# Casts of the down weights behind the last sine of the newest chunk, and last stores split by channel halves

## The chip, the cores and the metric

The kernel runs on one core of one Trainium2 chip. The metric is device time in microseconds from one launch to its end; a kernel's time is the median of its runs. The core has five engines that run side by side, each with its own instruction order: TensorE (matmul; weight loads are listed apart as PEld), VectorE (DVE), ScalarE (ACT), GpSimd (POOL) and SyncE (SP), which here only issues DMA transfers. ACT and POOL issue transfers too. Engines wait for each other through semaphores.

## The reference, cut to what matters

The input `x` has 2048 tokens of 448 channels. After a layer norm two branches are computed and added to `x`: a state-space convolution over the tokens (by FFT), and a gated linear unit.

```python
def _A_ref(u, log_A_real, A_imag, C_real, C_imag, log_dt, D_skip):
    dt = jnp.exp(log_dt)
    A = -jnp.exp(log_A_real) + 1j * A_imag
    C = (C_real + 1j * C_imag) * dt[:, None]
    P = jnp.exp((A * dt[:, None])[:, :, None] * pos[None, None, :])
    K = 2.0 * jnp.einsum("dn,dnl->dl", C, P).real
    Kf = jnp.fft.rfft(K, L2)
    Uf = jnp.fft.rfft(u_t, L2)
    y = jnp.fft.irfft(Uf * Kf[None, :, :], L2)[:, :, :L]
    return y + u * D_skip[None, None, :]

def _B_ref(x, w_gate, w_up, w_down):
    g = jnp.einsum("bsd,df->bsf", x, w_gate)
    u = jnp.einsum("bsd,df->bsf", x, w_up)
    h = _sigmoid(g) * u
    return jnp.einsum("bsf,fd->bsd", h, w_down)

xn = _layernorm(x, axis=-1)
return x + _A_ref(xn, ...) + _B_ref(xn, B_w_gate, B_w_up, B_w_down)
```

The hidden width of the gated unit is 1792, that is 14 tiles of 128, called f = 0 to 13 below.

## The kernel before, in words

Two Python generators write the program. `conv()` makes the convolution branch: norms and transposes of `x`, then `prep`, then `kgen` (the convolution kernel, in 56 chunks of 8 channels), then `spectra` (the products in the frequency domain and the way back). `glu()` makes the gated unit. The last lines of `s4d_glu_kernel` advance the generator that has done the smaller share of its total; a generator hands back, at each `yield`, how much work it counts. That gives the order in which instructions are traced. A scheduler then writes each engine's own order: among the instructions whose inputs are there it prefers those traced earlier. `hp(HP)` gives the instructions of a block a preference as if they had been traced 300 earlier. `tc.issue_after(ins)` puts what its block traces on the engine of `ins` behind `ins` in that engine's order; what the block traces on other engines is left alone.

**The gated unit.** Tokens go in two halves of 1024, each as two tiles `t` of 512. The f are taken in groups of 3, 3, 3, 3 and 2. For each f and t, `gate` multiplies the tokens by the gate and up weights (L709, each weight and input in a high and a low part: `wh`, `wl`, `xh`, `xl`; 11 matmuls for the gate and 11 for the up product), takes the tanh on ACT (`th`, L717, kept in `marks[0]`), multiplies on VectorE (`hf`, L720) and splits the result into `hh` (ACT, L725) and `hl` (VectorE, L727). At t = 0 the down weights of f are made ready. In the first half they are loaded (`rd`), rounded to the high part `dh` by a cast on ACT (L785), and POOL takes the rest `dl = rd - dh` (L786). The tiles that the second half will need again are stored by SyncE, except those of the f in `RAW` (f = 0, 1, 2, 4, 5). In the second half `dh` and `dl` come from there, or are made on POOL alone.

When all f of a group have been through their gates, 8 output blocks of 128 tokens follow (L825): three matmuls for each f, `hh` x `dh`, `hh` x `dl`, `hl` x `dh`, accumulated in one bank `po`, which VectorE adds to `acc` (L830). The banks of the gates (`gu`) and of the output blocks (`po`) share one tag with four buffers.

**The chunks.** `ahead(cn)` makes the phases of a chunk: two matmuls into `tr` (L542), then on ACT an absolute value (L548) and three sines (L549, L550, L551), into `S`. The last of them, L551, is kept in `sins`. POOL makes the magnitudes `me` and `mf` (L508, L520), VectorE multiplies them with the sines (`Et`, `Ft`, L602 to L604), and TensorE sums over the states (`ko`, L616). Chunk cn + 1's phases are traced ahead of chunk cn's products. The phases of chunk 0 are traced with high preference before the loop.

**The order around the change.** Run by the shares, the two generators trace the first `ahead` just before the cast of f = 5. For the casts of f = 5 to 13 the chunk traced last is 0, 0, 2, 5, 10, 12, 15, 20 and 22.

**The end.** The last group of the second half stores the output as it becomes ready. `out(src, b0, nb, ds, engs)` stores `nb` blocks from `b0`, channels `ds`, in four transfers (one for each 32 partitions), given in turn to the queues `engs`. `accs[2]` holds the blocks 8 to 11 and `accs[3]` (also `acc` at t = 1) the blocks 12 to 15. `H` is 224, half of the channels; `last(1, m)` adds the convolution's second half of channels to the output tiles, and at b = 3 that happens just ahead of the last stores.

Of the kernel before, what the change touches and what calls it, by code (L numbers as in the profile page):

```python
# [20 lines left out]
D = 448  # L21
# [15 lines left out]
HP = 300  # L37
Y0 = (8, 1)
CP = D // 4
H = D // 2  # L40
# [91 lines left out]
def s4d_glu_kernel(ctx, tc, io):  # L132
    nc = tc.nc
    hp = tc.high_priority
# [95 lines left out]
    accs = [acc_tile() for _ in range(2)]  # L230
# [230 lines left out]
    def kgen(pk):  # L461
# [73 lines left out]
        def ahead(cn):  # L535


            S = tl[f"S{cn % 2}"]
            ps = psc[-1].tile([128, 2, 512], F32, name="tr", bufs=1)
            ph = pht[cn // 2 % 2]  # L540
            for h in range(2):
                nc.tensor.matmul(ps[:, h], ph[:, cn % 2, 128 * h : 128 * h + 128], sel, start=True, stop=True)  # L542
            if cn % 2 == 1 and cn + 3 < NCK:
                phase_load(cn // 2 + 2)
            rows = lambda t: t.rearrange("p c (h e) s -> p h c (e s)", h=2)
            pv = ps.rearrange("p h (c x) -> p h c x", c=2)
            cs = S[:, 1:4:2]
            nc.scalar.activation(rows(cs), pv, AF.Abs)  # L548
            nc.scalar.activation(rows(S[:, 0:5:4]), pv, AF.Sin, scale=TWO_PI)  # L549
            nc.scalar.activation(rows(S[:, 2:3]), pv[:, :, 0:1], AF.Sin, scale=-TWO_PI)  # L550
            sins[:] = [nc.scalar.activation(cs, cs, AF.Sin, scale=-TWO_PI, bias=hpi)]  # L551
            return S

        def first_stage(bank):
# [175 lines left out]
    def glu():  # L730
        for half in range(2):
# [4 lines left out]
            for fs_ in ORDER[half]:  # L736
                fc, f0 = len(fs_), fs_[0]
                wts, ws, hs = [], [], [[], []]
                cross = half == 0 and fs_ is ORDER[0][-1]
                final = half == 1 and fs_ is ORDER[1][-1]  # L740

                order = [(f, t) for t in range(2) for f in fs_] if cross else [(f, t) for f in fs_ for t in range(2)]
                if half == 0 and f0 == 0:
                    order[1], order[2] = order[2], order[1]
                if cross:
                    xts = {b: pair_load(b) for b in range(8, 16, 2)}
                    step = lambda f_, b: f_(b, xts[b])
                    mid = [(pair_norm, 8), None, (pair_first, 8), (pair_first, 10)]
                    end = [(), ((pair_turn, 8), (pair_norm, 10)), ((pair_turn, 10), (pair_norm, 12)), ((pair_turn, 12), (pair_norm, 14))]
                    downs = {(0, 0): (pair_first, 12), (0, 1): (pair_turn, 14), (0, 3): (pair_first, 14)}  # L750
                for n_, (f, t) in enumerate(order):
                    if t == 0:
                        wh = pg.tile([128, 2, 4, 128], F32R, name="wh", bufs=2)
                        if half == 0:
                            first = len(raws) == 2
                            raw, rd = raws.pop() if raws else (w_load(f), None)
                            wl = w_low()
                            with hp(HP):
                                nc.scalar.copy(wh, raw)
                                if first:  # L760
                                    v.scalar_tensor_tensor(wl, raw, lim[:, 0, 0:1], wh, ALU.mult, ALU.subtract)
                                else:
                                    v.tensor_tensor(wl, raw, wh, ALU.subtract)
                            if f not in RAW:
                                for t_, d_ in kept((wh, wl), wt_d, f):
                                    nc.sync.dma_start(d_, t_)
                        elif f in RAW:
                            raw, wl = w_load(f, eng=nc.gpsimd), w_low()
                            nc.gpsimd.tensor_copy(wh, raw)  # L769
                            nc.gpsimd.tensor_tensor(wl, raw, wh, ALU.subtract)  # L770
                        else:
                            wl = w_low()
                            for t_, d_ in kept((wh, wl), wt_d, f):
                                nc.sync.dma_start(t_, d_)
                        ws.append((wh, wl))
                    between = (lambda s_=mid[n_]: step(*s_)) if cross and mid[n_] else None

                    yield from gate(ws[f - f0], xq[2 * half + t], hs[t], between, half == 0 and (f, t) == (1, 0))
                    if t == 0:
                        dh = pg.tile([128, D], F32R, name="dh", bufs=FCH[0])  # L780
                        if half == 0:
                            rd = rd or rd_load(f)
                            dl = d_low()
                            with hp(HP), tc.issue_after((act if f == 1 else marks)[0].ins):
                                nc.scalar.copy(dh, rd)  # L785
                            nc.gpsimd.tensor_tensor(dl, rd, dh, ALU.subtract)  # L786
                            if f not in RAW:
                                for t_, d_ in kept((dh, dl), dt_d, f):
                                    nc.sync.dma_start(d_, t_)
                        elif f in RAW:  # L790
                            dl = d_low()
                            rd = rd_load(f, pg.tile([128, D], F32, name="rdw", tag="wraw", bufs=1), nc.gpsimd)
                            nc.gpsimd.tensor_copy(dh, rd)  # L793
                            nc.gpsimd.tensor_tensor(dl, rd, dh, ALU.subtract)  # L794
                        else:
                            dl = d_low()
                            for t_, d_ in kept((dh, dl), dt_d, f):
                                nc.sync.dma_start(t_, d_)
                        wts.append((dh, dl))
                    yield 2.5  # L800
                    for s_ in end[n_] if cross else ():
                        step(*s_)
                    if cross:
                        yield 2
                for t in range(2):
                    acc = accs[2 * half + t]
                    for b in range(4):
                        if final and (t, b) == (0, 1):

                            yield None  # L810
                        if final and t == 1 and b >= 2:

                            sp_mm[:] = glu_mm
                            for m in (4 * b - 8, 4 * b - 6):
                                lasts[0](1, m)
                            if b == 3:
                                out(accs[2], 8, 4, slice(H, D), (nc.sync, nc.scalar))
                                out(accs[3], 12, 3, slice(0, D), (nc.sync, nc.scalar))
                        po = psg.tile([128, D], F32, name="po", tag="gu", bufs=4)
                        bs = slice(128 * b, 128 * b + 128)  # L820
                        n = 0
                        with tc.issue_after(sp_mm[0].ins) if glu_on else nullcontext():
                            for (hh, hl), (dh, dl) in zip(hs[t], wts):
                                for a_, w_ in ((hh, dh), (hh, dl), (hl, dh)):
                                    glu_mm[:] = [nc.tensor.matmul(  # L825
                                        po, a_[:, bs], w_, start=(n == 0), stop=(n == 3 * fc - 1)
                                    )]
                                    n += 1
                        with hp(HP):
                            v.scalar_tensor_tensor(  # L830
                                acc[:, b], po, 0.5, acc[:, b], ALU.mult, ALU.add
                            )
                        yield 0.6 * fc
                        if cross and (t, b) in downs:
                            step(*downs[t, b])
                    if cross:
                        nc.sync.dma_start(acc_d[:, 4 * t : 4 * t + 4], acc)
                    if final and t == 0:
                        out(acc, 8, 4, slice(0, H), (nc.gpsimd,))
                    elif final:  # L840
                        out(acc, 15, 1, slice(0, D), (nc.sync, nc.scalar))

    def spectra(pf):

# [260 lines left out]
        with tc.tile_pool(name="pf", bufs=1, side="right", reuse_waits="tile") as pf:  # L1105
            yield from spectra(pf)

    turns = []
    lasts, glu_mm, sp_mm, glu_on, x1s, hfs, xls = [], [], [], [], [0], [], []
    xq, psc, raws, acl, marks, slots, pqs = list(x_first), [], [], [], [None, None], {}, []  # L1110
    W1s, GGs, act, exps = [], [], [], []
# [43 lines left out]
```

## Time and profile before

| | us |
|---|---|
| median of 3 runs | 711.02 (710.64 to 714.73) |
| the profiled execution | 710.54 |
| its span, first to last instruction | 708.8 |
| mean granted TensorE clock | 0.988 of full speed |

The page gives for each engine its busy time and its share of the span. A row of the timeline has the start, the duration, the engine, the line of the kernel, the operation, the tiles written and read, their sizes, how many instructions the row merges, and in brackets the engine's idle time before them with the instruction that ended it. A row for a stretch of time has the busy time of TensorE, weight loads, VectorE, ACT and POOL, the granted clock, the share of the DMA engines and GB/s.

### The profile page before, as it was taken

The numbers are of one execution on the slowest core, as the hardware profiler recorded it, in microseconds if no ns is written. First come the engines' busy times: TensorE is split into PE (matmuls) and PEld (weight loads), VectorE is DVE, ScalarE is ACT, GpSimd is POOL, SyncE is SP. The second block draws the span as 40 slices with busy tenths as digits, with TensorE's granted clock in tenths as the row PEclk, the third lists the DMA queues.
The fourth block names the chain that finished last, engine by engine and source line by source line (L and its number), as shares of the span: only waits on it lengthen the run. The fifth ranks groups of instructions, "written<-read, shape, count | busy, mean of one in ns | idle before, by whom it ended". The sixth has DMA issues, their size and how long they took to land. (4 is left out here: it accounts for less than half of the span.)

```text
span 708.8 us, 19098 instructions
## 1 busy us (share of the span) xinstructions
PE 668.1 (94%) x7752; PEld 523.7 (74%) x7752; DVE 555.7 (78%) x766; ACT 428.7 (60%) x678; POOL 384.9 (54%) x433
## 2 busy tenths in 40 slices
PE   2798999999999998999999999999999999999996
PEld 2575878878877875756878878877777777777784
DVE  5899987699899998898478899988946555566544
ACT  3656965578689779877577788778543322322320
POOL 2101227655999999777446698798765001344001
PEclk9999999999999998989999999999999999999999
DMA  9956274554253544546833333242269988999756
GB/s 200 239 149 204 70 230 150 170 183 132 63 169 135 169 123 135 162 146 202 258 112 103 92 112 108 68 138 82 54 179 280 257 236 238 266 272 221 182 146 182
DMA packets 93031, 117.22 MB, mean 165 GB/s; under 512 B 12240, under 2 KB 76624, under 8 KB 92944
## 3 DMA queue, kind: packets, MB, share of 16 engines
q1 hardware_dynamic: 65376, 91.75, 46.3%
q10 hardware_dynamic: 24896, 18.13, 8.7%
q0 software_dynamic: 2672, 6.13, 3.2%
q8 instruction: 61, 1.00, 0.6%
q14 instruction: 26, 0.21, 0.1%
HBM read 72.13 MB, written 43.84 MB: 164 GB/s over the span
## 5 line engine op out<-in xcount | busy, mean ns | idle before, releaser
L520 POOL TENSOR_TENSOR me<-me,pm 128x32 f32<-128x32 f32 (+1 forms) x168 | 154.9, 922 | 66.8 <-DVE Et L603 38.1
L520 POOL TENSOR_TENSOR mf<-mf,pm 128x64 f32<-128x64 f32 (+1 forms) x112 | 116.9, 1044 | 5.1
L709 PE MATMUL gu<-xh,wh 128*128 128x512 f32 x336 | 100.1, 405 | 3.8 <-DVE acc L830 1.6
L709 PE MATMUL gu<-xh,wl 128*128 128x512 f32 x336 | 96.9, 393 | 0.0
L709 PE MATMUL gu<-xl,wh 128*128 128x512 f32 x336 | 95.1, 390 | 0.0
L602 DVE TENSOR_TENSOR Et<-me,S 128x1024 f32<-128x1024 f32 x56 | 80.2, 1433 | 11.6 <-ACT S L551 10.3
L825 PE MATMUL po<-dh,hh 128*128 128x448 f32 x224 | 84.2, 376 | 3.1 <-ACT hh L725 1.9
L548 ACT ACTIVATE S<-tr 128x1024 f32<-128x1024 f32 x56 | 57.7, 1030 | 44.9 <-PE tr L542 41.0
L604 DVE TENSOR_TENSOR Ft<-mf,S 128x1024 f32<-128x1024 f32 x56 | 80.1, 1431 | 5.3 <-PE ko L616 3.7
L603 DVE TENSOR_TENSOR Et<-me,S 128x1024 f32<-128x1024 f32 x56 | 80.4, 1436 | 4.8 <-ACT me L533 4.5
L825 PE MATMUL po<-dh,hl 128*128 128x448 f32 x224 | 82.4, 369 | 0.3 <-DVE hl L727 0.3
L825 PE MATMUL po<-dl,hh 128*128 128x448 f32 x224 | 82.3, 368 | 0.0
L709 PEld LDWEIGHTS gu<-xh,wh 128*128 128x128 f32 x336 | 60.8, 189 | 24.2 <-issue 4.4
L709 PEld LDWEIGHTS gu<-xh,wl 128*128 128x128 f32 x336 | 63.4, 189 | 14.7 <-DVE ve L255 0.7
L709 PEld LDWEIGHTS gu<-xl,wh 128*128 128x128 f32 x336 | 63.0, 188 | 13.5
L725 ACT CAST hh<-hf 128x512 fp32r<-128x512 f32 x56 | 34.9, 623 | 62.4 <-DVE hf L720 61.4
L616 PEld LDWEIGHTS ko<-Et,Ft 128*32 128x32 f32 x3584 | 54.7, 112 | 24.2 <-issue 13.4
L720 DVE SCALAR_TENSOR_TENSOR hf<-th,gu 128x512 f32<-128x512 f32 x56 | 38.1, 680 | 39.9 <-PE gu L709 35.2
L786 POOL TENSOR_TENSOR dl<-rd,dh 128x448 fp32r<-128x448 f32 x14 | 25.6, 1830 | 78.8 <-ACT dh L785 68.5
L616 PE MATMUL ko<-Et,Ft 128*32 128x64 f32 x3584 | 65.2, 223 | 2.6 <-DVE Ft L604 2.4
L551 ACT ACTIVATE S<-S,hpi 128x1024 f32<-128x1024 f32 x56 | 65.5, 1170 | 0.0
L717 ACT ACTIVATE th<-gu 128x512 f32<-128x512 f32 x56 | 33.5, 599 | 49.4 <-PE gu L709 43.0
(208 smaller groups left out, 1318.0 us busy)
## 6 DMA issues: line engine op xcount, KB each, us to landing
sk_d<-sk ACTq DMA_DIRECT2D x14, 512.0 KB
sx<-x_d SPq DMA_DIRECT2D x32, 224.0 KB
skl<-sk_d SPq DMA_DIRECT2D x16, 448.0 KB
vp<-v_d SPq DMA_DIRECT2D x16, 448.0 KB
v_d<-vt SPq DMA_DIRECT2D x14, 448.0 KB
ph<-ph_d SPq DMA_DIRECT2D x224, 24.0 KB
wt_d<-wh SPq DMA_DIRECT2D x9, 512.0 KB
wt_d<-wl SPq DMA_DIRECT2D x9, 512.0 KB
```

The lines of the kernel that those rows point to most:

```text
L520: ins = nc.gpsimd.tensor_tensor(m[:, :, w + a : 2 * w : n], m[:, :, a:w:n], par(base + i).unsqueeze(2).to_broadcast([128, 4 * DC, w // n]) ...
L548: nc.scalar.activation(rows(cs), pv, AF.Abs)
L551: sins[:] = [nc.scalar.activation(cs, cs, AF.Sin, scale=-TWO_PI, bias=hpi)]
L602: v.tensor_tensor(Et[:, :, :, 32:64], two(me[:, :, 32:64]), S[:, 1::-1], ALU.mult)
L603: v.tensor_tensor(Et[:, :, :, 0:32], two(me[:, :, 0:32]), S[:, 1:3, :, ::-1], ALU.mult)
L604: fts[:] = [v.tensor_tensor(Ft, two(mf), S[:, 3:5], ALU.mult)]
L616: mm = nc.tensor.matmul(ko[32 * j : 32 * j + 32, sl], Ft[:, cc, DC * h + 4 * q + j], Et[:, cc, DC * h + 4 * q + j], start=(k == 0), stop=( ...
L709: glu_mm[:] = [nc.tensor.matmul(ps, a_, b_, start=(n == 0), stop=(n == len(mm) - 1))]
L717: marks[0] = nc.scalar.activation(th, pgu[0], AF.Tanh, scale=0.5)
L720: marks[1] = v.scalar_tensor_tensor(hf, th, 1.0, pgu[1], ALU.add, ALU.mult)
L725: nc.scalar.copy(hh, hf)
L825: glu_mm[:] = [nc.tensor.matmul(po, a_[:, bs], w_, start=(n == 0), stop=(n == 3 * fc - 1))]
```

## The change

There are two parts.

First, `ahead` keeps its last sine in a list `newest` that all of the kernel sees. The cast `dh` (ACT) of the first half is now queued behind its gate's tanh for every f, and also behind the sine in `newest` if there is one. For f = 1 it stays behind the `xr` copy in `act`, with the tanh added.

Second, the last stores of `accs[3]` are cut otherwise. Before, blocks 12 to 14 went out with all channels ahead of the last output block's matmuls in the text, and block 15 after them, all on SyncE and ACT. Now the first half of the channels of blocks 12 and 13 is stored from POOL's queue as soon as block 13 is added; their second half goes out where blocks 12 to 14 went; and blocks 14 and 15 go out with all channels at the end.

```diff
             sins[:] = [nc.scalar.activation(cs, cs, AF.Sin, scale=-TWO_PI, bias=hpi)]
+            newest[:] = sins
             return S
...
-                            with hp(HP), tc.issue_after((act if f == 1 else marks)[0].ins):
+                            behind = act if f == 1 else newest or marks
+                            with hp(HP), tc.issue_after(marks[0].ins), tc.issue_after(behind[0].ins):
                                 nc.scalar.copy(dh, rd)
...
                                 out(accs[2], 8, 4, slice(H, D), (nc.sync, nc.scalar))
-                                out(accs[3], 12, 3, slice(0, D), (nc.sync, nc.scalar))
+                                out(accs[3], 12, 2, slice(H, D), (nc.sync, nc.scalar))
...
+                        if final and (t, b) == (1, 1):
+                            out(acc, 12, 2, slice(0, H), (nc.gpsimd,))
                         yield 0.6 * fc
...
                     elif final:
-                        out(acc, 15, 1, slice(0, D), (nc.sync, nc.scalar))
+                        out(acc, 14, 2, slice(0, D), (nc.sync, nc.scalar))
...
-    turns = []
+    turns, newest = [], []
```

## The prediction

> **What bounds the kernel now.** I read the page's busy table first, then busy time by stretches, then the order of work on ACT, POOL and TensorE around the casts of the down weights, and last the end of the run.
>
> ```profile
> PE 668.1 (94%) x7752; PEld 523.7 (74%) x7752; DVE 555.7 (78%) x766; ACT 428.7 (60%) x678; POOL 384.9 (54%) x433
> ```
>
> ```profile
> 110.00:150.00 40.00, 40.00 (x300) 33.63 (x298) 29.97 (x41) 25.35 (x35) 26.06 (x34) 1.00 0.53 166
> ...
> 200.00:250.00 50.00, 47.89 (x737) 39.24 (x737) 49.60 (x49) 39.83 (x58) 48.59 (x44) 1.00 0.52 163
> ```
>
> The columns of the second view are the length of the stretch, then PE, PEld, DVE, ACT and POOL busy, the granted clock, the DMA share and GB/s. TensorE is busy 668.1 of 708.8 us. From 110 to 150, where the first casts that the change moves lie, it has no idle time at all (40.00 of 40). So in that stretch a TensorE gap that the change opens is paid in full unless a later gap closes for it. From 200 to 250 VectorE is as full (49.60 of 50), and TensorE has gaps of 2.1 us.
>
> **Part 1: the casts.** A cast `dh<-rd` (L785) of `f` is today queued behind the tanh of its gate. Afterwards it is queued also behind the last sine of the newest chunk whose phases have been traced. Which chunk that is follows from the shares by which the two generators are advanced at the end of the kernel. For f = 0 to 4 no sine has been traced, so nothing changes (f = 1 was behind the last `xr` copy and gets its tanh added, which lies ahead of its cast anyway). For f = 5 to 13 the newest chunks are 0, 0, 2, 5, 10, 12, 15, 20 and 22. Only the last cast of each group of f can hold the group's output blocks, so f = 5, 8, 11 and 13 matter. The SyncE stores of `dh` and `dl` (f = 8 and 11) go later with their sources; nobody reads them before the second half.
>
> First f = 5, with ACT and then POOL:
>
> ```profile
> 105.49 0.59 ACT L717 ACTIVATE th<-gu 128x512 f32<-128x512 f32 x1
> 105.97 0.56 ACT L785 CAST dh<-rd 128x448 fp32r<-128x448 f32 x1
> ...
> 116.67 1.16 ACT L551 ACTIVATE S<-S,hpi 128x1024 f32<-128x1024 f32 x1
> 117.78 1.05 ACT L759 CAST wh<-wraw 128x1024 fp32r<-128x1024 f32 x1
> ```
>
> ```profile
> 106.61 1.24 POOL L786 TENSOR_TENSOR dl<-rd,dh 128x448 fp32r<-128x448 f32 x1 [0.60 <-ACT dh L785]
> ...
> 119.23 1.29 POOL L520 TENSOR_TENSOR mf<-mf,pm 128x64 f32<-128x64 f32 x1
> ```
>
> The cast ran at 105.97. The sine of chunk 0 starts at 116.67, and ACT takes its next instruction at 117.78. The cast gets that place: `dh` is there at 117.78 + 0.56 = 118.34. `dl` needs `dh` and follows on POOL, where the next instruction can start at 119.23: 119.23 + 1.24 = 120.47. The `wh` cast behind it goes 0.5 us later, and its gate comes two gates on, so that costs nothing. Who needs `dh` and `dl` of f = 5:
>
> ```profile
> 109.52 0.36 PE L825 MATMUL po<-dh,hh 128*128 128x448 f32 x1
> ...
> 110.94 0.36 PE L825 MATMUL po<-dl,hh 128*128 128x448 f32 x1
> 111.14 0.36 PE L825 MATMUL po<-dh,hh 128*128 128x448 f32 x1
> 111.35 0.36 PE L825 MATMUL po<-dh,hl 128*128 128x448 f32 x1
> ...
> 112.16 0.63 PE L542 MATMUL tr<-sel,ph 128*128 128x512 f32 x2
> ```
>
> The output blocks of f = 3, 4, 5 begin at 109.52, one matmul every 0.2 us (110.94, 111.14, 111.35). At 111.14 the next block's first matmul was put ahead of this block's last one, so the written order opens a further block when an operand of the open one is missing. The blocks share four PSUM buffers (tag `gu`). Each block has six matmuls without f = 5. Four blocks give 24 x 0.2 = 4.8 us, and the phase matmuls at 112.16 some 0.5: TensorE has work until about 109.5 + 5.3 = 114.8. Then all four buffers are held by blocks that lack f = 5, so no gate can start either. The phases of chunk 1 (0.6 us, as at 112.16) fit in once the sines have read the bank. Idle: 118.3 - 114.8 - 0.6 = 2.9. Four matmuls with `dh` take 0.8, to 119.1; the rest waits for `dl` until 120.5: 1.4. Together **4.3 us**. Bounds: 0, if the gates of f = 6 are ordered ahead of the blocks, and 8.3, if the order finishes the first block before the second (6 matmuls and 0.5 + 0.6 us of phases between 109.5 and 118.3, then 118.5 to 120.5). I take 4.3, because the row at 111.14 shows the interleaving.
>
> Then f = 8 and 11, on ACT and on TensorE:
>
> ```profile
> 156.79 0.58 ACT L785 CAST dh<-rd 128x448 fp32r<-128x448 f32 x1
> ...
> 162.52 1.17 ACT L551 ACTIVATE S<-S,hpi 128x1024 f32<-128x1024 f32 x1
> ...
> 219.77 0.56 ACT L785 CAST dh<-rd 128x448 fp32r<-128x448 f32 x1
> ...
> 230.73 1.18 ACT L551 ACTIVATE S<-S,hpi 128x1024 f32<-128x1024 f32 x1
> ```
>
> ```profile
> 162.49 0.36 PE L825 MATMUL po<-dh,hh 128*128 128x448 f32 x1
> ...
> 231.66 0.36 PE L825 MATMUL po<-dh,hh 128*128 128x448 f32 x1
> ```
>
> They move from 156.79 to 163.7 and from 219.77 to 231.9. With the cast (0.58) and a `dl` behind one POOL instruction (1.24 + 1.29) that is ready at about 166.8 and 235.0. The blocks begin at 162.49 and 231.66 and have 4.8 us of matmuls without the late f: covered to 167.3 and 236.5. **0** each, at worst some 1 us each; that cover is thin, and it is the only one. For f = 12 and 13 two whole gates lie between the cast and the first block: 0. What the casts leave free ahead of the sines (0.5 us at 219.77, with the next sines right behind it) buys nothing where VectorE is full.
>
> What comes back: TensorE's later waits for POOL and VectorE shrink when TensorE itself is late.
>
> ```profile
> 225.25 0.27 PE L566 MATMUL kp<-wk,ks 64*64 64x64 f32 x1 [0.91 <-POOL ks L627]
> ...
> 226.32 1.10 PE L616 MATMUL ko<-Et,Ft 128*32 128x64 f32 x64 [0.63 <-DVE Ft L604]
> ```
>
> These are 0.91 + 0.63 = 1.5 us. Since VectorE is nearly full before them and runs late too, I take **-1.0** of it (0 to -2.1, the whole idle of that stretch).
>
> Next the clock. In two neighbouring stretches of 6.8 us:
>
> ```profile
> 272.47:279.29 6.82, 4.82 (x82) 2.10 (x81) 6.82 (x10) 6.36 (x12) 6.51 (x7) 1.00 0.11 28
> 279.29:286.12 6.83, 6.83 (x76) 4.14 (x76) 4.54 (x4) 6.83 (x14) 6.67 (x10) 0.50 0.52 165
> ```
>
> TensorE was idle 2.0 us of the first one, and the granted clock was 0.50 all through the second. My 4.3 us of idle lie between 115 and 120.5, within about that length. So I expect one stretch at half clock, where 6.83 us do the work of 3.4: **+3.4** (0 without it, 6.8 for two).
>
> The Trainium skill, "TensorE: Matmul & The Clock Gate", section "HAM oscillation", gives the rule as "no PE-idle gaps >~3.4µs". Read by that rule, idle pieces of 2.9 and 1.4 us would not cost the clock, and the sum would lack the 3.4. The row disagrees with the rule read so: 2.0 us of idle in all came before the half clock.
>
> **Part 2: the last stores.**
>
> ```profile
> 701.12 4.48 SPq L239 DMA_DIRECT2D out_dram<-acc  x6
> ...
> 702.12 0.62 DVE L830 SCALAR_TENSOR_TENSOR acc<-po,acc 128x448 f32<-128x448 f32 x1 [0.50 <-PE po L825]
> ```
>
> ```profile
> 702.00:704.00 2.00, 0.09 (x1) 0.00 (x0) 0.62 (x1) 0.00 (x0) 0.00 (x0) 1.00 0.96 263
> 704.00:706.00 2.00, 0.00 (x0) 0.00 (x0) 0.00 (x0) 0.00 (x0) 0.00 (x0) 0.99 1.03 317
> ```
>
> The last addition ends at 702.74, and the DMA engines are full until 706 (0.96, 1.03). So bytes taken out of this stretch count. The first channel half of blocks 12 and 13 (2 x 128 x 224 x 4 B = 0.23 MB) goes to POOL's queue after the second block's addition, some 5 us earlier and beside matmuls; POOL has nothing else to do there. At 317 GB/s that is -0.72 us. Against it, the second half of these blocks is moved in pieces of 896 B, and the store that must wait for the last addition doubles to 0.46 MB: +0.72 us, were it alone on the engines. The number of issues on SyncE and ACT stays at six each. Bounds -0.7 and +0.7; I take **-0.4**, since the queues were still full of earlier stores at 704.
>
> The Trainium skill, "Perfetto Trace Analysis", section "DMA Optimizations", says that transfers below 2 KB carry a marked overhead each, which speaks against the halves. No row here separates piece sizes in this stretch.
>
> **Sum.** The profiled execution took 710.54 us (span 708.8 and 1.74 around it), 0.48 below the median of 711.02. 710.54 + 4.3 + 3.4 - 1.0 - 0.4 = 716.8; I say **717 us**.
>
> **Rivals.**
> - No half clock: the idle falls into two stretches of the clock's grid, or is too little. 717 - 3.4 = 713.4. The skill's rule above gives this case. Against it stands the row at 279.29.
> - The other side, no gap: the written order puts the two gates of f = 6 ahead of the blocks. Each has 22 matmuls of 512 columns, by the 0.2 us of 448 columns some 5 us, so two cover 109.5 to 118.3. Then only the stores are left: 710.5 - 0.7 = 709.8, faster than before by less than 1%. It decides from the point where the gates get two of the four `gu` buffers before the third block does. Against it: the blocks are traced first, and two of the buffers are free when they start.
> - A long gap: the order closes block after block, 8.3 us idle and one or two stretches at half clock: 710.5 + 8.3 + 3.4 to 6.8 - 1.4 = 721 to 724. For it: within a block the matmuls accumulate in order. Against it: the row at 111.14.
> - The change does nothing to the schedule, because the sine had been issued ahead of the cast anyway: so for f = 6, 7 and most others; for f = 5 the rows at 105.97 and 116.67 exclude it.
>
> **How the numbers follow.** Gap and half clock 0.42 (717, its own range 714.5 to 719); gap without it 0.22 (713.4); no gap 0.18 (709.8); long gap 0.16 (722); the rest 0.02. The range 709.5 to 721 reaches from the no-gap case into the long gap and leaves out about 2 in 10. About 1% is what a measurement of this kernel can tell from no change: below 703.9 or above 718.1. Faster 0.02. Slower: the long gap, 0.16, and a fifth of the likeliest case that lies above 718.1, together 0.25. Within 1%: 0.73.
>
> **What would show it.** Right: the cast of f = 5 directly behind the first L551 on ACT; TensorE idle before `po<-dh` at about 115 to 118 and before `po<-dl`; `dl` on POOL at about 119; a stretch of 6.8 us at clock 0.50 behind it; the last SyncE issues moving less after the last addition. Wrong: no TensorE wait for L785 or L786, gate matmuls between 110 and 118, a gap at 163 or 232 of more than 1 us, or a kernel below 709.

## The result, and the profile after

| | before | after |
|---|---|---|
| median, us (five runs of each, side by side) | 711.02 (709.6 to 714.8) | 737.75 (735.4 to 740.4) |
| ratio, with its 95% interval | | 1.0355 (1.0321 to 1.0388) |
| the profiled execution: time, span | 710.54, 708.8 | 737.75, 736.0 |
| mean granted clock | 0.988 | 0.971 |

The changed kernel is 3.6% slower, 27 us; the forecast was 717 with a range from 709.5 to 721. One execution of e1 below, the profiled one, was slow (1082 us at a granted clock of 0.56); it is left out of e1's numbers, and no trace of e1 is used. In the kernel after, the lines have moved down: the cast `dh` is L787, `dl` is L788, the output matmuls are L827, the additions L832, `ko` L617, the store of `dh` and `dl` L791. The sines (L548 to L551) and the phase matmuls (L542) have kept theirs.

**Where the time went.** Busy time by stretches, first of the kernel before, then after. The columns are as in the prediction: length, PE, PEld, DVE, ACT, POOL, clock, DMA share, GB/s.

```profile
105.00:145.00 40.00, 40.00 (x300) 33.85 (x299) 29.52 (x41) 23.84 (x35) 27.90 (x38) 1.00 0.50 159
145.00:185.00 40.00, 39.62 (x572) 32.74 (x575) 36.54 (x41) 32.02 (x46) 26.51 (x25) 1.00 0.47 144
185.00:265.00 80.00, 77.04 (x1192) 62.23 (x1182) 78.95 (x77) 64.01 (x91) 77.56 (x74) 1.00 0.46 136
265.00:365.00 100.00, 94.61 (x1349) 66.11 (x1348) 78.91 (x90) 77.90 (x126) 72.44 (x88) 0.93 0.59 178
```

```profile
105.00:145.00 40.00, 32.85 (x181) 26.37 (x180) 19.97 (x33) 19.75 (x28) 21.07 (x32) 0.87 0.38 117
145.00:185.00 40.00, 39.58 (x501) 31.72 (x503) 34.74 (x39) 25.03 (x36) 19.64 (x19) 1.00 0.50 163
185.00:265.00 80.00, 70.39 (x1056) 57.47 (x1047) 68.03 (x64) 60.58 (x89) 69.02 (x72) 0.94 0.39 120
265.00:365.00 100.00, 89.53 (x1270) 63.73 (x1269) 82.15 (x98) 79.67 (x125) 65.40 (x82) 0.93 0.48 143
```

TensorE was idle 0 + 0.4 + 3.0 + 5.4 = 8.7 us of these 260 before, and 7.2 + 0.4 + 9.6 + 10.5 = 27.7 after: 18.9 more. The stretches at half clock (those of the last microseconds left out, where TensorE has no work) add up to 13.7 us before, with TensorE busy all through them, and after to 41.0 us in seven stretches, of which TensorE was busy 31.2. At half clock the output matmuls follow each other after 0.37 us (at 126) instead of 0.20 (at 111), so about half of the busy part is lost. But the first of the seven, at 34.6 us with 6.1 busy, lies ahead of everything that the change moves, and e6 below, with no cast moved, has a half-clock stretch of 3.4 us at 34.9 too. The other six lose 12.5 us, against 6.8 before: 5.7 more. So of the 27.2 us of span, 18.9 are waits and 5.7 are clock between 105 and 365. The other 2.6 are not placed here; 1.2 of them lie ahead of the moved casts, since the output blocks of f = 3, 4, 5 began at 110.76 instead of 109.52.

VectorE lost 9.5 us of work in the first stretch (19.97 against 29.52). From 185 to 265 it was full in the kernel before (78.95 of 80). In the changed kernel it was not (68.03), so it is not shown that the lost work had no room to be made up.

Which waits they are stands in TensorE's waits from 105 to 365, of after (the longest five of nine groups; the columns are the total, the count and the longest):

```profile
PE po L827 <- POOL dl L788: 8.7, 2, 5.4
PE ko L617 <- DVE Ft L605: 6.7, 3, 4.5
PE gu L213 <- DVE xl L223: 5.2, 2, 4.4
PE ko L617 <- DVE Et L603: 3.4, 2, 2.5
PE tr L542 <- ACT S L550: 1.5, 3, 0.9
```

In the kernel before, no group in that stretch has more than 1.7, and none names `dl`.

**The first place, f = 5.** The orders of ACT, then TensorE, POOL and VectorE, all of the kernel after:

```profile
117.03 1.16 ACT L551 ACTIVATE S<-S,hpi 128x1024 f32<-128x1024 f32 x1
118.07 0.57 ACT L787 CAST dh<-rd 128x448 fp32r<-128x448 f32 x1
```

```profile
117.20 0.74 PE L542 MATMUL tr<-sel,ph 128*128 128x512 f32 x2 [0.95 <-ACT S L550]
118.69 1.08 PE L827 MATMUL po<-dh,hh 128*128 128x448 f32 x4 [0.75 <-ACT dh L787]
125.21 0.74 PE L827 MATMUL po<-dl,hh 128*128 128x448 f32 x1 [5.45 <-POOL dl L788]
```

```profile
114.11 0.31 POOL L520 TENSOR_TENSOR mf<-mf,pm 128x64 f32<-128x64 f32 x1
...
118.34 1.28 POOL L520 TENSOR_TENSOR me<-me,pm 128x32 f32<-128x32 f32 x1
119.58 1.28 POOL L520 TENSOR_TENSOR mf<-mf,pm 128x64 f32<-128x64 f32 x1
120.83 1.29 POOL L520 TENSOR_TENSOR me<-me,pm 128x64 f32<-128x64 f32 x1
...
123.45 0.62 POOL L520 TENSOR_TENSOR me<-me,pm 128x256 f32<-128x256 f32 x1
124.03 1.13 POOL L788 TENSOR_TENSOR dl<-rd,dh 128x448 fp32r<-128x448 f32 x1
```

```profile
119.41 1.29 DVE L604 TENSOR_TENSOR Et<-me,S 128x1024 f32<-128x1024 f32 x1
120.62 1.32 DVE L605 TENSOR_TENSOR Ft<-mf,S 128x1024 f32<-128x1024 f32 x1
...
126.37 1.37 DVE L832 SCALAR_TENSOR_TENSOR acc<-po,acc 128x448 f32<-128x448 f32 x2 [4.10 <-PE po L827]
```

The cast is where the forecast put it, and `dh` is there at 118.64. But `dl` starts only at 124.03, because POOL's order has seven magnitudes of the next pair of chunks between, from 118.34 on. The first three took 1.28 us each. The same form took 0.31 at 114.11; these three end just behind the three products of VectorE beside them (119.41 and 120.62 begin the second and third). TensorE stands 5.45 us, and VectorE, which waits for the blocks, 4.10.

The clock around it, from the stretch view:

```profile
113.09:119.92 6.83, 4.97 (x22) 3.50 (x20) 2.34 (x3) 6.61 (x10) 6.67 (x11) 1.00 0.65 192
119.92:130.16 10.24, 4.95 (x38) 3.95 (x38) 6.01 (x9) 3.72 (x5) 7.92 (x10) 0.50 0.29 99
```

The half clock began at 119.92, when TensorE had been idle 0.95, 0.75 and 0.16 us, before nearly all of the long wait. It lasted 10.24 us.

**Later places.** SyncE, ACT and TensorE around 230 (SPq and ACTq are transfers issued by the engine), and TensorE and POOL around the blocks of f = 9, 10, 11:

```profile
209.32 0.35 SPq L791 DMA_DIRECT2D dt_d<-dh  x1
221.81 0.35 SPq L791 DMA_DIRECT2D dt_d<-dl  x1
222.21 0.42 SPq L649 DMA_DIRECT2D rd<-in_B_w_down_dram  x1
222.72 5.07 SPq L492 DMA_DIRECT2D ph<-ph_d  x8
```

```profile
225.44 0.37 ACTq L575 DMA_DIRECT2D sk_d<-sk  x1
225.85 1.15 ACT L551 ACTIVATE S<-S,hpi 128x1024 f32<-128x1024 f32 x1 [5.27 <-DMA ph<-ph_d]
```

```profile
234.90 1.40 PE L617 MATMUL ko<-Et,Ft 128*32 128x64 f32 x44 [4.54 <-DVE Ft L605]
...
253.03 0.37 PE L827 MATMUL po<-dh,hh 128*128 128x448 f32 x1
256.62 0.74 PE L827 MATMUL po<-dl,hh 128*128 128x448 f32 x1 [3.22 <-POOL dl L788]
```

```profile
219.65 2.13 POOL L788 TENSOR_TENSOR dl<-rd,dh 128x448 fp32r<-128x448 f32 x1
...
254.45 2.12 POOL L788 TENSOR_TENSOR dl<-rd,dh 128x448 fp32r<-128x448 f32 x1
```

`dl` of f = 9 ran on POOL at 219.65. SyncE issues in order, so the store of that `dl` held its queue from 209.7 to 221.81, and the phase loads went behind it. ACT then stood 5.27 us at a store of its own, `sk_d`, which the trace has ended by the loads of `ph`. How that leads to TensorE's 4.54 us is not shown row by row: VectorE's own wait there, 2.49 us before 227.42, is put down to `mf` of POOL. At 253 TensorE waits for `dl` of f = 11 itself.

**The end.** The last addition and the last issues on SyncE:

```profile
730.25 0.62 DVE L832 SCALAR_TENSOR_TENSOR acc<-po,acc 128x448 f32<-128x448 f32 x1 [0.50 <-PE po L827]
```

```profile
728.71 3.65 SPq L239 DMA_DIRECT2D out_dram<-acc  x6
```

From the end of the last addition to the end of the span it is 736.0 - 730.87 = 5.1 us, where it was 708.8 - 702.74 = 6.1.

### The profile page after: what moved, and what is told of

It is laid out like the page before. It is cut to its first block, busy times and chain, and to the rows that moved or that the text cites. A ratio compares the mean times of both kernels' runs of the same rounds, so it can differ in the third digit from the quotient of the medians.

```text
span 736.0 us, 19106 instructions
## 1 busy us (share of the span) xinstructions
PE 678.8 (92%) x7752; PEld 531.5 (72%) x7752; DVE 552.3 (75%) x766; ACT 429.5 (58%) x678; POOL 372.1 (51%) x437
## 5 line engine op out<-in xcount | busy, mean ns | idle before, releaser
L520 POOL TENSOR_TENSOR me<-me,pm 128x32 f32<-128x32 f32 (+1 forms) x168 | 144.1, 858 | 90.1 <-DVE Et L604 51.1
L520 POOL TENSOR_TENSOR mf<-mf,pm 128x64 f32<-128x64 f32 (+1 forms) x112 | 118.9, 1062 | 4.5
L710 PE MATMUL gu<-xh,wl 128*128 128x512 f32 x336 | 98.7, 398 | 0.0
L827 PE MATMUL po<-dl,hh 128*128 128x448 f32 x224 | 84.1, 376 | 8.7 <-POOL dl L788 8.7
L548 ACT ACTIVATE S<-tr 128x1024 f32<-128x1024 f32 x56 | 57.8, 1031 | 52.4 <-PE tr L542 50.8
L827 PE MATMUL po<-dh,hh 128*128 128x448 f32 x224 | 84.4, 379 | 2.3 <-DVE acc L832 1.2
L827 PE MATMUL po<-dh,hl 128*128 128x448 f32 x224 | 83.9, 375 | 0.3 <-DVE hl L728 0.3
L617 PEld LDWEIGHTS ko<-Et,Ft 128*32 128x32 f32 x3584 | 56.2, 113 | 33.8 <-issue 14.7
L617 PE MATMUL ko<-Et,Ft 128*32 128x64 f32 x3584 | 67.5, 225 | 11.5 <-DVE Ft L605 7.8
L832 DVE SCALAR_TENSOR_TENSOR acc<-po,acc 128x448 f32<-128x448 f32 x80 | 48.4, 616 | 29.0 <-PE po L827 28.8
L551 ACT ACTIVATE S<-S,hpi 128x1024 f32<-128x1024 f32 x56 | 65.5, 1170 | 5.4 <-DMA ph<-ph_d 5.3
L788 POOL TENSOR_TENSOR dl<-rd,dh 128x448 fp32r<-128x448 f32 x14 | 24.1, 1722 | 87.4 <-ACT dh L787 87.4
```

Of the source, the lines that this page charges most:

```text
L520: ins = nc.gpsimd.tensor_tensor(m[:, :, w + a : 2 * w : n], m[:, :, a:w:n], par(base + i).unsqueeze(2).to_broadcast([128, 4 * DC, w // n]) ...
L617: mm = nc.tensor.matmul(ko[32 * j : 32 * j + 32, sl], Ft[:, cc, DC * h + 4 * q + j], Et[:, cc, DC * h + 4 * q + j], start=(k == 0), stop=( ...
L710: glu_mm[:] = [nc.tensor.matmul(ps, a_, b_, start=(n == 0), stop=(n == len(mm) - 1))]
L827: glu_mm[:] = [nc.tensor.matmul(po, a_[:, bs], w_, start=(n == 0), stop=(n == 3 * fc - 1))]
L832: v.scalar_tensor_tensor(acc[:, b], po, 0.5, acc[:, b], ALU.mult, ALU.add)
```

## The experiments

All are built from the kernel before, and each ratio is to runs of that kernel on the same chip (its median was 711.5 to 713.1 there).

| run | what is in it | median, us | ratio (95%) |
|---|---|---|---|
| e1 | stores alone | 713.50 | 0.9992 (0.9961 to 1.0024) |
| e2 | all casts late | 740.08 | 1.0371 (1.0313 to 1.0429) |
| e3 | cast of f = 5 late | 730.18 | 1.0231 (1.0185 to 1.0277) |
| e4 | casts of f = 6 to 13 late | 715.71 | 1.0034 (1.0007 to 1.0062) |
| e5 | e2, dh and dl stored from POOL | 732.67 | 1.0277 (1.0226 to 1.0327) |
| e6 | before, dh and dl stored from POOL | 713.11 | 1.0012 (0.9963 to 1.0060) |
| e7 | e3, dh and dl stored from POOL | 729.06 | 1.0229 (1.0184 to 1.0275) |
| e8 | e3, dl of f = 5 first on POOL | 725.42 | 1.0171 (1.0117 to 1.0226) |
| e9 | e2, every dl first on POOL | 723.08 | 1.0145 (1.0110 to 1.0181) |
| e10 | e2, ACT's stores from POOL | 743.82 | 1.0424 (1.0367 to 1.0481) |
| e11 | before, ACT's stores from POOL | 729.07 | 1.0195 (1.0126 to 1.0265) |
| e12 | e5, rd loaded from POOL too | 730.03 | 1.0245 (1.0181 to 1.0309) |
| e13 | before, only dl late | 727.27 | 1.0189 (1.0137 to 1.0240) |
| e14 | e2, dl of f = 5 first on POOL | 717.64 | 1.0067 (1.0046 to 1.0088) |

**The two parts apart (e1, e2).** e1 has the three `out` lines of the diff, e2 the edge.

> The stores' part alone. Theory (the loss lies in the casts, the stores are worth some tenths of a microsecond): 709.5 to 711.5 us, with the first 0.23 MB leaving on POOL's queue some 5 us earlier and the span's end 0 to 0.8 us sooner. Rival (the stores cost by their smaller pieces or the doubled last store): 713 us or more.

> The casts' part alone. Theory (the casts hold all of the loss): 734 to 741 us, like the whole change. Rival (the stores hold a part of it): below 730 us.

The stores make no difference that can be told (713.5 is above e1's own forecast, but the kernel before took 712.9 beside it), and the casts alone cost what the whole change costs.

**The casts apart (e3, e4).**

```diff
-                            behind = act if f == 1 else newest or marks
+                            behind = act if f == 1 else newest if f == 5 else marks
+                            behind = act if f == 1 else newest if f > 5 else marks
```

The removed line is that of e2. The first of the added lines is that of e3, the second that of e4.

> The casts' part for f = 5 alone; f = 6 to 13 stay behind their tanh. Theory (every late cast costs by itself): TensorE again idle some 7 us between 115 and 126 and about 10 us at half clock behind it, 718 to 724 us, and after 140 us no gap above 2 us that the kernel before lacks. Rival (the first gap throws the order of everything behind it, the later casts add nothing): 733 us or more.

> The casts' part for f = 6 to 13 alone; f = 5 stays behind its tanh. Theory (the later casts cost by themselves, through SyncE's queue and through late dl on POOL): no gap at 115 to 126, gaps of 3 to 5 us as at 230, 253 and 300 to 340 in the whole change, 722 to 730 us. Rival (all comes from the first gap): 709 to 714 us.

Neither theory fits. f = 5 alone costs 16 us, more than the other eight casts together by far (2.4), and the two do not add up to the 26 of e2. e3 shows where its later loss begins, on SyncE and ACT:

```profile
174.87 0.33 SPq L791 DMA_DIRECT2D dt_d<-dl  x1
175.24 4.30 SPq L492 DMA_DIRECT2D ph<-ph_d  x8
...
180.74 1.13 SPq L643 DMA_DIRECT2D wraw<-in_B_w_up_dram  x2
```

```profile
183.49 1.04 ACT L760 CAST wh<-wraw 128x1024 fp32r<-128x1024 f32 x1 [4.58 <-DMA wraw<-in_B_w_up_dram]
```

The casts behind f = 5 are not moved in e3, and still the store of the `dl` of f = 8 holds SyncE's queue until 174.87, the weight loads behind it come late, ACT stands 4.58 us at the cast of the weights, the sine behind that is late, and TensorE is idle 3.85 us before the next phase matmuls. But a held queue is nothing new. In the kernel before, the two stores of f = 8 on SyncE, and its `dl` on POOL:

```profile
157.40 0.34 SPq L789 DMA_DIRECT2D dt_d<-dh  x1
163.60 0.34 SPq L789 DMA_DIRECT2D dt_d<-dl  x1
```

```profile
161.44 2.14 POOL L786 TENSOR_TENSOR dl<-rd,dh 128x448 fp32r<-128x448 f32 x1
```

There the queue stood 5.9 us, from 157.74 to 163.60, with phase and weight loads behind it, and no gap of TensorE followed (39.62 us of 40 busy from 145 to 185). In e3 it stood 4.4 us, from 170.47 to 174.87. So the hold alone does not cost; that the loads behind it are needed sooner in e3 is likely, not shown.

**SyncE's queue freed (e5, e6, e7).**

```diff
                                 for t_, d_ in kept((dh, dl), dt_d, f):
-                                    nc.sync.dma_start(d_, t_)
+                                    nc.gpsimd.dma_start(d_, t_)
```

> All casts behind the newest sine as in the changed kernel, and the stores of dh and dl for the second half on POOL's own queue instead of SyncE's (last stores as before). Theory (these stores stop SyncE's queue while dl is late, and the loads of phases and weights stand behind them): the 4.5 us TensorE gap at about 230 goes, ph is not loaded late there, and the time falls from 740 to 724-733, because the first gap at 115 to 125 stays. Rival (the loads are late for other reasons, or TensorE then waits for dl itself): 737-743, with gaps of the same total behind 125.

> The kernel before with only the stores of dh and dl moved from SyncE's queue to POOL's. It is the control for the runs with that move: both theories expect 709-715, since the stores behind an early dl hold nothing up; POOL pays for some ten issues beside other work.

> Only the cast of f = 5 is late, and the stores of dh and dl go through POOL's queue. Theory (the 3.85 us gap at 183 and the ones behind it come from SyncE's queue held by the store of a late dl): no gap of over 1.5 us between 130 and 230, time 718-726 instead of 730. Rival (TensorE's lateness of some 12 us behind the first gap reshuffles the work on VectorE and ACT, with or without the stores): 728-732.

The control costs nothing. With all casts late the stores on POOL bring back some 7 us (1.0371 to 1.0277), but the gap near 230 is still there with 2.6 us, and one of 4.0 at 245: the loads of `rd`, whose buffer comes free with `dl`, still stand in front of the phase loads. With f = 5 alone the gap at 183 falls from 3.85 to 0.6 us, as the theory has it, but the time stays, as the rival has it: gaps of 1.7 at 187, 2.0 at 241 and 2.4 at 289 take its place. So the held queue is a real step of the chain, and freeing it alone gives little.

**POOL's order (e8, e9, e14).** The magnitudes that are traced after a `dl` are queued behind it on POOL; e8 and e14 do so for f = 5, e9 for f = 5 to 13.

```diff
-            with tc.issue_after(mls[0].ins) if mls else nullcontext():
+            with tc.issue_after(low5[0].ins) if low5 else nullcontext(), tc.issue_after(mls[0].ins) if mls else nullcontext():
...
-                            nc.gpsimd.tensor_tensor(dl, rd, dh, ALU.subtract)
+                            low = nc.gpsimd.tensor_tensor(dl, rd, dh, ALU.subtract)
+                            if f == 5:
+                                low5[:] = [low]
```

> Only the cast of f = 5 is late, and POOL's magnitudes traced after its dl are queued behind that dl. Theory (the 5.4 us TensorE wait for dl is POOL's order, seven magnitudes ahead of it): dl runs at about 118.7 instead of 123, the wait shrinks to under 1.5 us, the half clock behind it to 6.8 us or less, and the time to 715-723. Rival (the lateness of the block of output matmuls matters little, and what costs is the other order that the scheduler writes behind a late cast): the gap shrinks and the time stays at 726-731.

> All casts late (last stores as before), and POOL's magnitudes that are traced after a dl are queued behind that dl, for f = 5 to 13. Theory (the lateness of dl on POOL is what holds SyncE's queue, and through it ACT and VectorE; the cast itself is cheap): dl follows its dh within 2 us nearly everywhere, the TensorE waits for dl at 120 and 253 fall under 1.2 us, the gap at 230 goes, and the time falls from 740 to 716-727. Rival (the order that the scheduler writes behind late casts costs whatever dl does): 730 or more, with new gaps of the same total.

> All casts late, and POOL's magnitudes behind dl for f = 5 alone, the other dl as the scheduler puts them. Theory (the first gap with its half clock, and SyncE held by the dl of f = 8 and later, cost about equally): TensorE's wait for dl at 119 is 0.8 us, the gap near 230 is back with 3 us or more, time 727-733, between 723 (all dl first) and 740 (none). Rival (the first gap starts everything): 720-725.

In e8 the wait for `dl` fell from 5.4 to 0.8 us and no half clock followed, but the time went down by only 4 to 5 us, between the two forecasts. VectorE of e8 lost nothing from 105 to 145:

```profile
105.00:145.00 40.00, 37.57 (x285) 30.62 (x284) 30.93 (x40) 26.39 (x38) 28.55 (x37) 1.00 0.43 141
```

So e8 is still some 12 us slower than the kernel before (1.0171) with neither the long wait nor the lost work of VectorE. In e14 all casts stay where the change puts them, and one edge on POOL brings the ratio from 1.0371 to 1.0067, that is 22 us back. POOL and TensorE of e14:

```profile
117.84 1.78 POOL L788 TENSOR_TENSOR dl<-rd,dh 128x448 fp32r<-128x448 f32 x1 [0.61 <-ACT dh L787]
```

```profile
117.82 1.86 PE L829 MATMUL po<-dh,hh 128*128 128x448 f32 x4 [0.76 <-ACT dh L787]
119.68 0.74 PE L829 MATMUL po<-dl,hh 128*128 128x448 f32 x1
```

The wait for `dl` is gone, and VectorE has its work of the first stretch back (30.46 us from 105 to 145):

```profile
105.00:145.00 40.00, 38.05 (x225) 30.72 (x226) 30.46 (x40) 25.82 (x36) 28.55 (x37) 0.96 0.42 131
```

This ran lower than both theories had it, although the gap near 230 is still there with 3.50 us. Three things warn against reading the 22 us as the price of the first place. The same edge takes 22 us off e2 and only 4 to 5 off e3. e8 has the same first place, fewer late casts, and takes some 7 us more than e14. And e9, where every `dl` is early and the theory's number held, takes 5 to 6 us more than e14: TensorE's waits for `Ft` sum to 10.5 us there, since the magnitudes now stand behind the late casts (at 174.87 VectorE waits 1.55 us for `me` of POOL). The scheduler writes another order behind every edge, and that the order alone is worth several us is the likely reason, not a shown one.

**dl late, the casts early (e13).**

```diff
-                            nc.gpsimd.tensor_tensor(dl, rd, dh, ALU.subtract)
+                            with tc.issue_after(newm[0].ins) if f > 4 and newm else nullcontext():
+                                nc.gpsimd.tensor_tensor(dl, rd, dh, ALU.subtract)
```

(`newm` holds the last magnitude on POOL.)

> The kernel before with the casts where they were, and only dl of f = 5 to 13 (POOL) queued behind the last of POOL's magnitudes traced before it. Theory (what costs is the lateness of dl, on TensorE at once and on SyncE's queue later): the first wait for dl opens at about 114 to 118, gaps of 1.5 to 4 us follow between 200 and 340, and the time is 717-732. Rival (the casts' place among ACT's sines is what costs): 708-715.

The theory's range held. The cast is at 106.3 as before, `dl` runs at 116.97, TensorE waits 1.31 us for it, and the time is up 14 us all the same. The next loss looks like that of e3, step by step:

```profile
167.44 0.33 SPq L791 DMA_DIRECT2D dt_d<-dl  x1
167.81 4.18 SPq L492 DMA_DIRECT2D ph<-ph_d  x8
...
173.18 1.13 SPq L643 DMA_DIRECT2D wraw<-in_B_w_up_dram  x2
```

```profile
175.98 1.04 ACT L760 CAST wh<-wraw 128x1024 fp32r<-128x1024 f32 x1 [4.49 <-DMA wraw<-in_B_w_up_dram]
```

TensorE is idle 3.7 us there, from 175.7. As in e8, a loss of more than 10 us comes behind a first wait that is short, so it may come from another order as such.

**Three that tell little (e10, e11, e12).** In e10 and e11 `sk_d` and the pairs' `x_d` are stored from POOL's queue instead of ACT's; e12 is e5 with `rd_load` of f above 4 from POOL's queue.

> All casts late, and the stores that ACT issues in this stretch (sk_d, and x_d of the pairs) go through POOL's queue. Theory (ACT stands still at these issues until SyncE's held loads have run, and that makes the gaps at 230 and 311): ACT has no idle time of over 3 us before a sine between 200 and 320, and the time falls from 740 to 724-735; the first gap stays. Rival (ACT's stop is not what VectorE and TensorE wait for): 736-745.

> The control: the kernel before with the same stores of sk_d and x_d through POOL's queue. Both theories expect 707-717: in the kernel before SyncE's queue is seldom held, and POOL pays some thirty issues beside other work.

> All casts late, and nothing on SyncE waits for dl any more: the stores of dh and dl and also the loads of rd (whose buffer comes free with dl) go through POOL's queue. The run with the stores alone kept the gap at 231, with rd now in front of the phase loads. Theory (SyncE held by whatever waits for dl): no phase load is issued behind a dl, the gaps at 231 and 245 shrink to under 1.5 us, time 720-729. Rival (the phase loads are late for their own buffer): 729-735 as with the stores alone.

The control e11 went up some 14 us by itself (1.0195; TensorE's longest waits there from 105 to 365 are for `Ft`, 5.8 us, `xl`, 2.9, and `ks`, 2.8), so e10 does not settle whether ACT's stop at `sk_d` is what costs around 230: its trace has waits of 1.13 and 2.58 us for VectorE at 238 and 245 in place of the 4.54, and its time is no lower. e12's median lies just inside its rival's range, and its interval reaches into both; the gap that was to fall under 1.5 us is 3.6 at 241, and the one at the first place 5.4.

## Why the prediction was wrong

- **The place of the cast: right.** It went directly behind the first L551, at 118.07 (forecast 117.78), and TensorE stood before the phases and before `po<-dh` for 1.7 us (2.9 forecast). The order of the blocks was the interleaved one, so neither "no gap" nor the block-after-block order of "long gap" came about; a long gap came from POOL instead.
- **The failed step: `dl` "follows on POOL, where the next instruction can start at 119.23", with nothing charged for what comes after.** The place on POOL was read off the old order, as if `dl` came next as soon as `dh` was there. It came behind seven magnitudes, at 124.03, and the wait was 5.45 us instead of 1.4. The old order had a warning: in the kernel before, `dl` of f = 8 to 11 starts 4.1 to 5.8 us after the end of its cast (161.44 against 157.37 for f = 8), not behind one POOL instruction. Still, at the first place the sum is only 2 us short: 7.2 idle and 2.5 of clock, 9.7, where 4.3 + 3.4 = 7.7 were forecast. Some 17 of the 27 us come elsewhere, nearly all of them later, and there the sum had 0 for f = 8 and 11 and -1.0 for later waits. Early `dl` in e14 (117.84) gives 717.6, in e8 (117.43) 725.4. That e14 lands near the forecast's 717 is luck: its 3.50 us before 235.56 are not in the forecast.
- **The half clock: right in kind, too small.** One stretch of 6.8 us was forecast; it was 10.24 at the first place, with 4.95 us of work in it (2.5 lost), and from 105 us on 5.7 us more were lost to it than before, instead of 3.4. The Trainium skill, "TensorE: Matmul & The Clock Gate", section "HAM oscillation", has the half clock follow TensorE gaps above some 3.4 us. The trace disagrees again: it set in behind pieces of 0.95, 0.75 and 0.16 us.
- **"-1.0 comes back": wrong in sign.** TensorE being late did not shorten later waits: from 105 to 365 those for `Ft` rose from 1.3 to 6.7 us, those for `xl` of L223 from 1.5 to 5.2. VectorE also lost 9.5 us of work at first, but e8 shows that later losses come without that.
- **"The SyncE stores go later with their sources; nobody reads them": wrong.** Nobody reads the stores, but what is queued behind them is read. In the changed kernel the queue stood 12.1 us for f = 9, against 6.6 before (190.95 to 197.58), and ACT stood 5.27 us until the phase loads behind it had run. In e3 and e13 loads come late behind the store of f = 8 too, but there the queue stood no longer than before.
- **f = 8 and 11 at 0, under 4.8 us of cover: f = 8 right, f = 11 wrong.** The blocks at 251.82 were closed one after the other, so TensorE reached the `dl` of f = 11 after seven matmuls and waited 3.22 us. `dl` itself started 3.9 us after the end of its cast (250.51).
- **The stores: right.** The last stretch became 0.9 us shorter in the profiles (0.4 forecast), which the timed runs cannot tell from nothing.
- **A slip in the sum of the bounds.** By its own terms the long gap comes to 6.5 + 2.0 = 8.5 us, not 8.3; this changes no conclusion.

**What stays open.** The waits of the first place with their clock are some 10 us of the 27 (7.2 idle, 2.5 clock), and their cause is shown: the late cast, and POOL's order, since e8 and e14 take the 5.45 us away. The cause of the other 17 is open. A late `dl` alone costs 14 us (e13), and putting it first gives 22 back in e14, but only 4 to 5 in e8. The held queue of SyncE is one way, but freeing it gave 7 us in e5 and nothing in e7. The rival is that another order costs whatever `dl` does, since the scheduler writes a new one behind every edge. For it, e11 moves only stores and is 14 us slower; against it, e4 and e6 change the order too and cost 2.4 us and nothing that can be told. No run separates the two; e8 against e14 puts the accident of the order at 7 us or more. No kernel here is faster than the one before.

## What to carry to other kernels

Moving an instruction later on one engine moves its successors on other engines too, and there they do not go to the next slot: look for what the scheduler has ready to put ahead of them, and force the successor's place if it matters. Before costing a late store at nothing, list what stands behind it in its queue and how soon that is needed. And do not price an edge by its first gap alone: here that gap was forecast within 2 us, and the loss behind it was nearly twice as large. When the same edge gives 22 us in one kernel and 4 to 5 in its neighbour, the order is part of the price.

## What the hardware showed

- POOL's small products take four times as long beside VectorE's products of two inputs in SBUF: 1.28 us instead of 0.31 for 128x64, each ending just behind the VectorE instruction beside it. The Trainium skill, "SBUF — State Buffer", section "Who interferes with whom", has a VectorE instruction with two SBUF inputs contend with a GpSimd instruction that reads SBUF. The trace agrees: the three products of POOL end 0.1 to 0.2 us behind the VectorE products beside them.
- Whether idle time of 2.4 us costs the clock is not fixed. In e8 the pieces 0.89, 0.76 and 0.79 us lie between 115.0 and 119.3, and the clock stays. In e9 they are 0.90, 0.76 and 0.78 us, and 3.4 us at half clock begin at 119.2. In e14 1.19 and 0.76 us lie at about the same place, and a stretch of 3.4 us follows at half. The half-clock stretches of these traces are 3.41, 6.83, 10.24 or 13.65 us long, multiples of one length, so where the pieces fall on such a grid may decide; that is not shown. In the 3.4 us ahead of the half clock TensorE was busy 1.80 us in e9 and 1.57 in e14, but 2.16 in the kernel before (275.88 to 279.29). The stretches of e8, then of e14:

```profile
117.70:121.10 3.40, 2.61 (x13) 2.10 (x13) 3.40 (x3) 3.40 (x5) 3.40 (x3) 1.00 0.25 61
```

```profile
117.71:121.12 3.41, 3.30 (x8) 2.48 (x9) 3.41 (x3) 3.41 (x6) 3.28 (x3) 0.50 0.21 56
```
